# Token-major router scores and PSUM rank arithmetic in a fused attention and mixture-of-experts kernel

## The chip, the cores and the metric

One core of one Trainium2 chip runs the whole program as one launch. The metric is the device time of that launch in microseconds (us); lower is better. A kernel is timed several times, and the median stands for it. A profile is one further execution with the hardware profiler on.

## What is computed

Sparse attention in two kinds of heads, then a top-1 mixture of experts with a skip test:

```python
# attention: 8 batches, 8 heads, 576 tokens, head size 64
rel = pos[:, None] - pos[None, :]
mask_local   = (rel >= 0) & (rel < 32)                          # heads 0-3
mask_strided = (rel >= 0) & (pos[None, :] % 32 == pos[:, None] % 32)   # heads 4-7
attn = softmax(where(mask, q @ k.T / 8, -1e9)) @ v
x = attn.transpose(0, 2, 1, 3).reshape(4608, 512)
# router and experts: 8 experts, 512 -> 1024 -> 512
do_compute = x @ w_skip > 0
logits = x[do_compute] @ w_gate
e_idx  = argmax(logits); gate_w = softmax(logits)[e_idx]
y = gate_w * (relu(x @ w1[e_idx]) @ w2[e_idx])
out = x;  out[do_compute] = x + y
```

Everything is float32. The output is the attention result with the expert's result added in the rows that the skip test lets through.

## The kernel before

**Units.** The work of a batch's attention is cut into four units, `UNITS`: two of the local kind (`kind` 0, blocks of 64 tokens: five and four of them) and two of the strided kind (`kind` 1, eleven blocks of 54 tokens: three residues of 32 with 18 tokens each, in groups of six and five). A loop over `n` goes through the 32 units, `n = 4*b + pr` for batch `b` and unit `pr`. Below, (b, 2) is the iteration with `pr = 2` of batch `b`.

**One unit** passes through five steps that are Python generators; a `yield` parts what is issued on one engine from what is issued on the next:

- `qk` (line 199): TensorE computes the scores into the one PSUM tile `S`; VectorE adds the mask (line 206 for the local kind into `sm`, 208 for the strided kind into the one buffer `sms`); VectorE takes the maximum (214); GpSimd subtracts it (217).
- `tex` (237, 245): TensorE transposes, ScalarE takes the exponential out of a PSUM tile `T`, of which there are four.
- `pv` (271 to 286): TensorE multiplies with the values into the one PSUM tile `PV`; VectorE divides by the sum.
- `xpose` (313, 315): TensorE transposes the result, ScalarE copies it to `xT_[b, kind]`, one buffer for each kind. In the local kind the columns are tokens in order; in the strided kind they are `residue * 18 + token // 32`.
- `store`: the result goes to the output in DRAM.

Iteration n runs `qk` for unit n+2, `tex` for unit n, `pv` for unit n-1 and `xpose` for unit n-2, in the order that the loop body writes. The orders of TensorE, VectorE and GpSimd are those of the program; ScalarE's order is chosen by the scheduler that lays out the program.

**Routing one batch.** A batch is a group `g`, 576 tokens in five tiles of 128 (`GT`). Its steps are woven into the iterations of the next batches:

- `score` (329, 333, 334) at (b, 2) for batch b-1: for each half batch, TensorE multiplies the nine router columns `w9`, padded to 64, as the stationary operand with the transposed values as the moving one. The two kinds give two partial sums in two halves of the partitions, because their tokens are ordered differently. ScalarE copies both into `s64`, the second with a stride that restores the token order.
- `route1` at (b, 3): five TensorE transposes (349) turn `s64` token-major, ScalarE copies the one part (351), VectorE adds the other (355), and nine short VectorE operations (358 to 373) choose the expert and count.
- `route2` at (b+1, 0): TensorE prefix sums with triangular and full matrices of ones (400 to 406) give each token its rank in its expert; VectorE picks it (411, 412) into `rank_`.
- `norm`, `gates` (382 to 394): the softmax value of the chosen expert, on GpSimd, split into three bf16 parts; one reciprocal on VectorE (390).
- `hot`: four VectorE operations on five columns (430 to 433) cut the rank into quotient `hq` and remainder `hc` by 3, and two wide ones make one-hot matrices (435, 438); `mul` (446) on GpSimd multiplies one of them by the parts.
- `place` (456): TensorE adds up a table of which token goes where, and VectorE accumulates it (460, 462).

A table `plan` gives the iterations of `gates`, `hot`, `mul` and `place` for each group:

```python
plan = {x: (4 * x + 8, 4 * x + 10, 4 * x + 10, 4 * x + 12) for x in range(CB - 1)}
plan[CB - 1] = (4 * CB + 4, 4 * CB + 5, 4 * CB + 5, 4 * CB + 7)
plan[CB] = (4 * CB + 8, 4 * CB + 7, 4 * CB + 8, 4 * CB + 9)
plan[CB + 1] = (None, 4 * CB + 11, None, None)
```

With `CB = 5`, group 5 has `hot` at n = 27, `gates` and `mul` at 28 and `place` at 29. For the late batches, b = 6 and 7, `route1` and `route2` both run at (b, 3).

**The turn to the experts.** At n = 29, (7, 1), the table of groups 0 to 5 is complete; `tabled` (467 to 472) turns it into lists of tokens, and GpSimd starts an indirect gather (624) of up to 288 rows for one expert, called "e", whose weights are fetched during attention. After the loop TensorE transposes these rows (`xturn`, 646), and expert "e" starts (`ffn1a`, 691 to 695, then `ffn1`, 652 to 654) while the last batch is routed between its matrix products. Then the other seven experts follow.

Of the kernel before, what the change touches and what calls it, by code (L numbers as in the profile page):

```python
# [21 lines left out]
ST = 32  # L22
# [39 lines left out]
def _cols():  # L62
    at = 0
    for name, n in (("id", 128), ("ml", 5 * LW), ("ms", SQ), ("w8", NE), ("pk", 2 * NT), ("io", 128),
                    ("key", NE), ("e8", NE), ("cap", NE), ("ov", NOV),
                    ("eh", 24)):
        _C[name] = (at, at + n)
        at += n
    return at
# [5 lines left out]
def make_consts():  # L75
    c = np.zeros((128, C_END), np.float32)

    def put(name, a):
        c[:, slice(*_C[name])] = a

    put("id", np.eye(128))
    ml = np.zeros((128, 5, LW))
    i, w = np.arange(128)[:, None] % HP, np.arange(LW)[None, :]
    for t in range(5):
        ml[:, t] = np.where((i + 1 <= w) & (w <= i + ST) & (w >= (ST if t == 0 else 0)), 0.0, BIG)
    w = np.arange(SQ)[None, :]
# [4 lines left out]
    pk = np.zeros((128, NT, 2))  # L91
    for (a, z), o, o2 in zip(GROUPS, GOFF, GOFF[1:]):
# [13 lines left out]
def attn_moe(ctx: ExitStack, tc: tile.TileContext, q, k, v, w9d, w1d, w2d, cst, out, NB=B):  # L106
# [11 lines left out]
    ident = con["id"]  # L118
    w9 = constp.tile([128, 4, 64], F32, name="w9")
    tri = constp.tile([128, 128], BF16, name="tri")  # L120
# [10 lines left out]
    def ps(tag, n=1):  # L131
        return psum.tile([128, n, 512] if n > 1 else [128, 512], F32, name=tag, tag=tag, bufs=bufs[tag])
# [7 lines left out]
    def setup():  # L140
        fill = constp.tile([128, NE, 4], I32, name="fill")
        V.tensor_scalar(tri, con["io"], con["pk"][:, 0:1], None, op0=ALU.is_ge)
        V.memset(oneb, 1.0)
        V.memset(runs[0], 0.0)
        V.memset(s64[:, S:GT * 128], 0.0)
# [171 lines left out]

    rt_ = {}
    s64 = ap.tile([64, GT * 128], F32, name="s64")

# [3 lines left out]

    def score(b, h, tag="T"):
        p = ps(tag)
        for i in range(2):
            for kind in range(2):
                T.matmul(p[64 * kind:64 * kind + 64, 0:288], lhsT=w9[:, 2 * kind + i, :],
                         rhs=xT_[b, kind][:, i, h * 288:(h + 1) * 288], start=(i == 0), stop=(i == 1))  # L330
        yield
        at = (b - [g for g in GROUPS if g[0] <= b < g[1]][0][0]) * S
        A.copy(s64[0:32, at + h * 288:at + (h + 1) * 288], p[0:32, 0:288])
        A.copy(s64[32:64, at:at + S].rearrange("p (a r) -> p r a", r=ST)[:, 16 * h:16 * h + 16, :],
               p[64:96, 0:288].rearrange("p (r a) -> p r a", a=NA))

    def route1(g, tag="T"):
# [7 lines left out]

        sc = ps(tag)
        scv = sc[:, 0:nt * 41].rearrange("p (t c) -> p t c", c=41)
        for t in range(nt):
            T.transpose(scv[:, t, :], s64[0:41, t * 128:(t + 1) * 128], ident[:41, :41])
        s9 = sp("s9", [128, nt, 9])  # L350
        A.copy(s9, scv[:, :, 0:9])
        yield
        o = slice(GOFF[g], GOFF[g + 1])
        w8 = con["w8"].unsqueeze(1).broadcast_to([128, nt, NE])
        V.tensor_tensor(s9, scv[:, :, 32:41], s9, op=ALU.add)
        lg = s9[:, :, 1:9]
        m = sp("rm", [128, nt])
# [9 lines left out]

        V.scalar_tensor_tensor(mw, s9[:, :, 0], 0.0, mw, op0=ALU.is_gt, op1=ALU.mult)
        ohb = sp("rohb", [128, nt, NE], BF16)
# [26 lines left out]
    def route2(g, tag="T", of=None):  # L396
        nt, sp, ohb, o, _ = rt_[g]
        rk = ps(tag)
        rkv = rk[:, 0:nt * NE].rearrange("p (t e) -> p t e", e=NE)
        T.matmul(rkv, lhsT=tri, rhs=ohb, start=True, stop=False)  # L400
        yield
        for t in range(nt - 1):
            T.matmul(rkv[:, t + 1:nt, :], lhsT=oneb,
                     rhs=ohb[:, t:t + 1, :].broadcast_to([128, nt - 1 - t, NE]), start=False, stop=False)
            yield
        T.matmul(rkv, lhsT=oneb, rhs=runs[g % 2].unsqueeze(1).broadcast_to([128, nt, NE]), start=False, stop=True)
        if of is not None:
# [4 lines left out]
        V.tensor_reduce(rank_[:, o], dd, axis=AX.X, op=ALU.add)  # L412
        if of is not None:
            counted(of)
# [8 lines left out]
    def hot(g):  # L423
        o = slice(GOFF[g], GOFF[g + 1])
# [5 lines left out]
        V.tensor_scalar(q, rank_[:, o], -1.0, 1.0 / 3.0, op0=ALU.add, op1=ALU.mult)  # L430
        V.tensor_scalar(q, q, MAGIC, -MAGIC, op0=ALU.add, op1=ALU.add)
        V.tensor_tensor(c, q, pickw[:, o], op=ALU.add)
        V.scalar_tensor_tensor(c, c, -3.0, rank_[:, o], op0=ALU.mult, op1=ALU.add)
        eh = sp("heh", [24], BF16)
# [7 lines left out]
    def mul(g):  # L442
# [5 lines left out]
        hot_[g] = lo, pm  # L448

    hot_ = {}  # L450

# [391 lines left out]
    plan[CB - 1] = (4 * CB + 4, 4 * CB + 5, 4 * CB + 5, 4 * CB + 7)  # L843
    plan[CB] = (4 * CB + 8, 4 * CB + 7, 4 * CB + 8, 4 * CB + 9)
    plan[CB + 1] = (None, 4 * CB + 11, None, None)
    pool_order = ExitStack()
    pool_order.enter_context(tc.manual_schedule(engines={G.engine, T.engine, V.engine}))
    for n, (b, pr) in enumerate(units):
# [37 lines left out]
        if ranked is not None:  # L886
            rank = [route2(ranked, of=COUNTED.get(b - 1))]
# [13 lines left out]
        late = []  # L901
        if b > 0 and pr == 2:
            seq = [score(b - 1, 0), score(b - 1, 1)] + seq
        if n > 1 and not (g and pr == 2):
            seq.append(xpose(*units[n - 2]))
        run(*seq)
        if not full:
            run(*put)
        if g and pr == 3:
            norm(g[0])  # L910
        if g and pr == 2:
            late = [route1(g[0])]
        if g and pr == 3:
# [16 lines left out]
        for x, it in plan.items():  # L930
            for f, at in zip((hot, gates, mul), (it[1], it[0], it[2])):
                if at == n:
                    f(x)
# [12 lines left out]
    nr = len(GROUPS) - 1  # L946
    gates(CB + 1)
    mul(CB + 1)
    engines = ExitStack()
# [14 lines left out]
    wrest("e", 3, 5)  # L964
    run(score(NB - 1, 0), score(NB - 1, 1))
    g = ffn1("e", 2, 6)
# [140 lines left out]
def pack(inputs):  # L1107
# [23 lines left out]
    w9 = np.concatenate([np.asarray(inputs["moe_w_skip"])[:, None], np.asarray(inputs["moe_w_gate"])], axis=1)  # L1131
    w9 = np.pad(w9.reshape(4, 128, 9).transpose(1, 0, 2), ((0, 0), (0, 0), (0, 55)))
    w1 = np.asarray(inputs["moe_w1"]).reshape(NE, 4, 128, 4, 256).transpose(0, 3, 2, 1, 4).reshape(NE, 4, 128, 1024)
# [29 lines left out]
```

## Time and profile before

| quantity | value |
|---|---|
| median of 3 timed runs | 451.05 us (447.95 to 451.74) |
| time of the profiled execution | 453.04 us |
| span of the profiled execution, first to last instruction | 451.3 us |
| mean granted TensorE clock | 0.976 |
| busy: TensorE, VectorE, ScalarE, GpSimd | 412.4, 280.9, 186.4, 142.6 us |
| attention loop | from the start to about 177 us |
| experts | from about 182 us to the end |

The profile has views of one execution. The time line lists instructions by start time: start, duration, engine (PE is TensorE, PEld its weight loads, DVE is VectorE, ACT is ScalarE, POOL is GpSimd), line of the kernel, operation, output and inputs, how many instructions were merged into the row, and in brackets how long the engine had stood idle before and what ended that. A row of the windows gives the busy time of each engine in a stretch, the granted TensorE clock, the share of the DMA engines and their rate. A row of the groups sums all instructions of a line. Names lose their trailing digits, so `w9` and `s64` appear as `w` and `s`. "issue" as a releaser means that nothing that the profile shows held the engine.

### The profile page before, as it was taken

How to read it: one execution, taken by the hardware profiler on the slowest of the kernel's cores; microseconds unless marked ns; L12 is line 12 of the kernel's file. 1: busy time of each engine (PE TensorE's matmuls, PEld its weight loads, DVE VectorE, ACT ScalarE, POOL GpSimd, SP SyncE). 2: the span in 40 equal slices, each digit the busy share in tenths (PEclk: the TensorE clock that was granted, in tenths of full speed). 3: DMA queues.
4: the chain of work that ended last, by engine and by line, in shares of the span. 5: the costliest groups of instructions: out<-in, count | busy, mean ns of one | idle time of the engine just before them, and what ended most of it. 6: DMA issues, size and time to landing. Idle time of an engine off the chain costs nothing.

```text
span 451.3 us, 12196 instructions
## 1 busy us (share of the span) xinstructions
PE 412.4 (91%) x4991; PEld 370.0 (82%) x4992; DVE 280.9 (62%) x606; ACT 186.4 (41%) x370; POOL 142.6 (32%) x200
## 2 busy tenths in 40 slices
PE   5989899799889667999899999999999999999994
PEld 3866768587677556789799799999999999999984
DVE  2666798969987876781377465365484564755611
ACT  1334443436345316642443243444444444544400
POOL 2434445344454355034014327012224023200201
PEclk9799999999989979999999999999999999999999
DMA  8999989979893134515347466546566466655201
GB/s 287 388 393 315 350 276 343 326 227 352 265 377 120 43 101 153 172 69 141 91 155 212 155 201 205 167 153 187 187 199 186 152 209 192 210 159 169 61 20 42
DMA packets 51805, 90.38 MB, mean 200 GB/s; under 512 B 8251, under 2 KB 27963, under 8 KB 51745
## 3 DMA queue, kind: packets, MB, share of 16 engines
q1 hardware_dynamic: 45249, 79.19, 52.8%
q0 software_dynamic: 6496, 10.37, 8.0%
q8 instruction: 40, 0.66, 0.6%
q14 instruction: 20, 0.16, 0.1%
HBM read 75.16 MB, written 14.91 MB: 200 GB/s over the span
## 4 chain that ended last, share of the span: by engine, by line
PE 50%; DMA 2%; POOL 0%; DVE 0%; POOLq 0%; issue 0%
PE S L652 15%; PE S L654 15%; PE S L653 15%; PE PV L744 2%; DMA xg<-out_dram,tab 2%; PE T L646 1%; PE PV L786 0%; PE PV L784 0%; PE PV L785 0%; PE S L760 0%; PE S L759 0%; PE S L761 0%; POOL out_dram L732 0%; PE T L771 0%; PE S L646 0%; PE PV L646 0%
## 5 line engine op out<-in xcount | busy, mean ns | idle before, releaser
L652 PE MATMUL S<-xh,w1h 128*128 128x342 f32 (+6 forms) x248 | 78.6, 317 | 0.2 <-DVE hl L665 0.2
L654 PE MATMUL S<-xh,w1l 128*128 128x342 f32 (+6 forms) x248 | 76.7, 309 | 0.0
L653 PE MATMUL S<-xl,w1h 128*128 128x342 f32 (+6 forms) x248 | 76.6, 309 | 0.0
L732 POOL DMA_INDIRECT out_dram<-ot,tab x25 | 28.0, 1122 | 150.0 <-DVE ot L730 141.8
L652 PE MATMUL S<-hh,w2h 128*128 128x288 f32 (+5 forms) x192 | 59.4, 310 | 0.5 <-DVE hl L665 0.5
L654 PE MATMUL S<-hh,w2l 128*128 128x288 f32 (+5 forms) x192 | 58.0, 302 | 0.0
L653 PE MATMUL S<-hl,w2h 128*128 128x288 f32 (+5 forms) x192 | 57.9, 302 | 0.0
L664 ACT ACTIVATE hh<-S 128x342 fp32r<-128x342 f32 (+6 forms) x64 | 28.0, 437 | 64.0 <-PE S L654 58.3
L588 DVE TENSOR_TENSOR w1l<-raw,w1h 128x1024 fp32r<-128x1024 f32 x32 | 39.0, 1223 | 20.0 <-ACT w1h L582 20.0
L199 PE MATMUL S<-kt,qt 64*64 64x54 f32 (+1 forms) x1280 | 34.3, 247 | 14.9 <-DVE sms L208 5.0
L652 PEld LDWEIGHTS S<-xh,w1h 128*128 128x128 f32 x248 | 46.9, 189 | 0.9 <-issue 0.4
L653 PEld LDWEIGHTS S<-xl,w1h 128*128 128x128 f32 x248 | 46.8, 189 | 0.1
L654 PEld LDWEIGHTS S<-xh,w1l 128*128 128x128 f32 x248 | 46.7, 188 | 0.0
L199 PEld LDWEIGHTS S<-kt,qt 64*64 64x64 f32 x1280 | 28.3, 145 | 22.2 <-issue 7.3
L217 POOL TENSOR_TENSOR sm<-sm,mx 128x480 f32<-128x480 f32 (+1 forms) x32 | 28.5, 911 | 55.8 <-DVE mx L214 29.3
L624 POOL DMA_INDIRECT xg<-out_dram,tab x25 | 33.7, 1347 | 36.8 <-issue 14.4
L588 DVE TENSOR_TENSOR w2l<-raw,w2h 128x1024 fp32r<-128x1024 f32 x32 | 39.1, 1223 | 9.8 <-ACT w2h L582 9.6
L665 DVE SCALAR_TENSOR_TENSOR hl<-S,hh 128x342 fp32r<-128x342 f32 (+6 forms) x64 | 30.9, 483 | 17.8 <-ACT hh L664 17.7
L652 PEld LDWEIGHTS S<-hh,w2h 128*128 128x128 f32 x192 | 36.1, 188 | 0.8 <-DVE hl L665 0.8
L315 ACT COPY xT<-T 128x512 f32<-128x512 f32 (+4 forms) x56 | 22.2, 441 | 35.0 <-PE T L313 34.8
L649 DVE TENSOR_TENSOR xl<-T,xh 128x288 fp32r<-128x288 f32 (+7 forms) x30 | 13.1, 468 | 37.3 <-ACT xh L648 37.2
L653 PEld LDWEIGHTS S<-hl,w2h 128*128 128x128 f32 x192 | 36.3, 189 | 0.0
(180 smaller groups left out, 828.3 us busy)
## 6 DMA issues: line engine op xcount, KB each, us to landing
raw<-in_w_dram SPq DMA_DIRECT2D x64, 512.0 KB
vt<-in_vp_dram SPq DMA_DIRECT2D x40, 390.0 KB
qt<-in_qp_dram SPq DMA_DIRECT2D x16, 304.0 KB
kt<-in_kp_dram SPq DMA_DIRECT2D x16, 297.0 KB
out_dram<-x SPq DMA_DIRECT2D x16, 288.0 KB
kt<-in_kp_dram SPq DMA_DIRECT2D x14, 304.0 KB
qt<-in_qp_dram SPq DMA_DIRECT2D x14, 288.0 KB
out_dram<-x SPq DMA_DIRECT2D x32, 99.0 KB
```

Of the source, the lines that this page charges most:

```text
L199: T.matmul(s[HP * (i ^ j):HP * (i ^ j) + HP, j, (blk - b0) * win:(blk - b0 + 1) * win], lhsT=qt[p, j, blk * nq:blk * nq + HP], rhs=kt[p, j ...
L217: G.tensor_tensor(e[:, j], sw[:, j], mx[:, j].unsqueeze(2).broadcast_to([128, b1 - b0, win]), op=ALU.subtract)
L315: A.copy(xT_[b, kind][:, :, g * nq:(g + m) * nq].rearrange("p i (n q) -> p n i q", q=nq), t[:, 0:m * 128].rearrange("p (n i q) -> p n i q" ...
L588: V.tensor_tensor(lo, raw_.pop((key, j)), hi.bitcast(F32), op=ALU.subtract)
L624: i = G.indirect_dma_start(out=xg[:s["P"], t, :], out_offset=None, in_=out[0:last, :], in_offset=bass.IndirectOffsetOnAxis(ap=s["tab"][:s[ ...
L649: V.tensor_tensor(xl[:, c, :C], t[:, :C], xh[:, c, :C].bitcast(F32), op=ALU.subtract)
L652: T.matmul(p, lhsT=a[0], rhs=b[0], start=start, stop=False)
L653: T.matmul(p, lhsT=a[0], rhs=b[1], start=False, stop=False)
L654: T.matmul(p, lhsT=a[1], rhs=b[0], start=False, stop=stop)
L664: A.activation(s["hh"][:, f, :C], p[:, :C], AF.Relu)
L665: V.scalar_tensor_tensor(s["hl"][:, f, :C], p[:, :C], 0.0, s["hh"][:, f, :C].bitcast(F32), op0=ALU.max, op1=ALU.subtract)
L732: i = G.indirect_dma_start(out=out, in_=ot[:P], in_offset=None, bounds_check=NTOK - 1, oob_is_err=False, out_offset=bass.IndirectOffsetOnA ...
```

## The change

**Scores.** `score` and `s64` are gone. `xpose` writes the local kind into `xT_` in the strided kind's token order, with two strided copies for each group of blocks where there was one. `route1` multiplies directly: for each of the five tiles the transposed values are the stationary operand (128 columns, 64 in the last tile) and the nine router columns the moving one, four products of 128 rows summed in PSUM over the two kinds. VectorE reads the scores from PSUM. The table of token numbers `pk` follows the new order.

**Ranks.** The operations that cut the rank into quotient and remainder move from `hot` to the end of `route2`. Their intermediate values stay in the PSUM tile of the ranks, and ScalarE copies the rank and the quotient to SBUF.

**Iterations.** Group 5 has `gates`, `hot` and `mul` all at n = 27, group 6 all at n = 31 (`gates` and `mul` stood behind the loop). For b = 6 and 7 `route1` runs at the end of (b, 2) and `route2` within (b, 3).

```diff
-        pk[:, o:o2, 0] = 1 + np.arange(128)[:, None]
-        pk[:, o:o2, 1] = a * S // 64 + 2 * np.arange(o2 - o)[None, :]
+        pk[:, o:o2, 0] = 1 + (a * S + at) % 64
+        pk[:, o:o2, 1] = (a * S + at) // 64
...
     def xpose(b, pr):
...
-            A.copy(xT_[b, kind][:, :, g * nq:(g + m) * nq].rearrange("p i (n q) -> p n i q", q=nq),
-                   t[:, 0:m * 128].rearrange("p (n i q) -> p n i q", i=2, q=HP)[:, :, :, 0:nq])
+            t = t[:, 0:m * 128].rearrange("p (n i q) -> p n i q", i=2, q=HP)
+            if kind:
+                A.copy(xT_[b, 1][:, :, g * nq:(g + m) * nq].rearrange("p i (n q) -> p n i q", q=nq), t[:, :, :, 0:nq])
+                continue
+            for i in range(2):
+                A.copy(xT_[b, 0][:, i, :].rearrange("p (r n h) -> p n h r", r=ST, h=2)[:, g:g + m],
+                       t[:, :, i, :].rearrange("p n (h r) -> p n h r", r=ST))
...
-    def score(b, h, tag="T"):
-        ...
     def route1(g, tag="T"):
...
+        sc = ps(tag)[:, 0:nt * 9].rearrange("p (t c) -> p t c", c=9)
         for t in range(nt):
-            T.transpose(scv[:, t, :], s64[0:41, t * 128:(t + 1) * 128], ident[:41, :41])
-        s9 = sp("s9", [128, nt, 9])
-        A.copy(s9, scv[:, :, 0:9])
+            n = min(128, S - 128 * t)
+            if n < 128:
+                T.matmul(sc[n:128, t, :], lhsT=dummy[:, n:128], rhs=dummy[:, 0:9], start=True, stop=True)
+            for c in range(4):
+                T.matmul(sc[0:n, t, :], lhsT=xT_[g, c // 2][:, c % 2, 128 * t:128 * t + n], rhs=w9[:, c, :], start=(c == 0), stop=(c == 3))
         yield
-        V.tensor_tensor(s9, scv[:, :, 32:41], s9, op=ALU.add)
-        lg = s9[:, :, 1:9]
+        lg = sc[:, :, 1:9]
...
     def route2(g, tag="T", of=None):
...
-        dd = sp("rdd", [128, nt, NE])
+        dd = rk[:, 64:64 + nt * NE].rearrange("p (t e) -> p t e", e=NE)
+        r, a, q, c = [rk[:, 128 + 16 * i:128 + 16 * i + nt] for i in range(4)]
+        hq, hc = [ap.tile([128, GT], F32, name=n, tag=n, bufs=2) for n in ("hq", "hc")]
         V.tensor_tensor(dd, rkv, ohb, op=ALU.mult)
-        V.tensor_reduce(rank_[:, o], dd, axis=AX.X, op=ALU.add)
+        V.tensor_reduce(r, dd, axis=AX.X, op=ALU.add)
+        A.copy(rank_[:, o], r)
+        V.tensor_scalar(a, r, -1.0, 1.0 / 3.0, op0=ALU.add, op1=ALU.mult)
+        V.tensor_scalar(q, a, MAGIC, -MAGIC, op0=ALU.add, op1=ALU.add)
+        A.copy(hq, q)
+        V.tensor_tensor(c, q, pickw[:, o], op=ALU.add)
+        V.scalar_tensor_tensor(hc, c, -3.0, rank_[:, o], op0=ALU.mult, op1=ALU.add)
+        hot_[g] = hq, hc
...
     def hot(g):
-        q, c = sp("hq", []), sp("hc", [])
-        V.tensor_scalar(q, rank_[:, o], -1.0, 1.0 / 3.0, op0=ALU.add, op1=ALU.mult)
-        V.tensor_scalar(q, q, MAGIC, -MAGIC, op0=ALU.add, op1=ALU.add)
-        V.tensor_tensor(c, q, pickw[:, o], op=ALU.add)
-        V.scalar_tensor_tensor(c, c, -3.0, rank_[:, o], op0=ALU.mult, op1=ALU.add)
+        q, c = hot_[g]
...
-    plan[CB] = (4 * CB + 8, 4 * CB + 7, 4 * CB + 8, 4 * CB + 9)
-    plan[CB + 1] = (None, 4 * CB + 11, None, None)
+    plan[CB] = (4 * CB + 7, 4 * CB + 7, 4 * CB + 7, 4 * CB + 9)
+    plan[CB + 1] = (4 * CB + 11, 4 * CB + 11, 4 * CB + 11, None)
...
-        if b > CB:
-            run(*late)
-            late = []
...
-        if b > 0 and pr == 2:
-            seq = [score(b - 1, 0), score(b - 1, 1)] + seq
...
         if g and pr == 2:
             late = [route1(g[0])]
-        if g and pr == 3:
-            if b > CB:
-                run(route2(g[0], of=COUNTED.get(b)))
-            else:
-                ranked = g[0]
+        if g and pr == (2 if b > CB else 3):
+            run(*late)
+            late = []
+            norm(g[0])
+            ranked = g[0]
...
-    gates(CB + 1)
-    mul(CB + 1)
...
-    run(score(NB - 1, 0), score(NB - 1, 1))
```

More of the change, by code (lines that the diff above doesn't have):

```diff
@@ L63, in _cols @@
     at = 0
-    for name, n in (("id", 128), ("ml", 5 * LW), ("ms", SQ), ("w8", NE), ("pk", 2 * NT), ("io", 128),
+    for name, n in (("id", 128), ("ml", 5 * LW), ("ms", SQ), ("w8", NE), ("pk", 2 * NT), ("ip", 1), ("io", 128),
                     ("key", NE), ("e8", NE), ("cap", NE), ("ov", NOV),
@@ L118, in attn_moe @@
     ident = con["id"]
-    w9 = constp.tile([128, 4, 64], F32, name="w9")
+    w9 = constp.tile([128, 4, 9], F32, name="w9")
     tri = constp.tile([128, 128], BF16, name="tri")
@@ L314, in xpose @@
             yield
-            A.copy(xT_[b, kind][:, :, g * nq:(g + m) * nq].rearrange("p i (n q) -> p n i q", q=nq),
-                   t[:, 0:m * 128].rearrange("p (n i q) -> p n i q", i=2, q=HP)[:, :, :, 0:nq])
+            t = t[:, 0:m * 128].rearrange("p (n i q) -> p n i q", i=2, q=HP)
[5 more added lines that the diff above has]
+                       t[:, :, i, :].rearrange("p n (h r) -> p n h r", r=ST))
     rt_ = {}
-    s64 = ap.tile([64, GT * 128], F32, name="s64")
     def tiles(g):
         return GT
-    def score(b, h, tag="T"):
[L326 to L335, printed above, removed]
+    hot_ = {}
     def route1(g, tag="T"):
@@ L448, in mul @@
         hot_[g] = lo, pm
-    hot_ = {}
     def place(g, tag="T"):
@@ L886, in attn_moe @@
         if ranked is not None:
-            rank = [route2(ranked, of=COUNTED.get(b - 1))]
+            rank = [route2(ranked, of=COUNTED.get(b if pr else b - 1))]
             for _ in range(tiles(ranked) + 1):
@@ L930, in attn_moe @@
         for x, it in plan.items():
-            for f, at in zip((hot, gates, mul), (it[1], it[0], it[2])):
+            for f, at in zip((gates, hot, mul), it):
                 if at == n:
```

15 lines of the change are left out of this document (6 added, 9 removed).

## The prediction, made before the changed kernel ran

> **What bounds the kernel now.** First the page, for span and clock, then windows cut by batch, then the time line.
>
> ```profile
> span 451.3 us, 12196 instructions
> ...
> PEclk9799999999989979999999999999999999999999
> ...
> 63.00:82.00 19.00, 17.54 (x402) 14.02 (x396) 16.66 (x44) 8.89 (x23) 9.70 (x18) 1.00 0.95 319
> ...
> 145.00:167.00 22.00, 14.02 (x328) 11.88 (x322) 16.64 (x48) 7.69 (x18) 10.52 (x18) 0.91 0.29 80
> ```
>
> A batch takes some 19 us, the last ones 22. After the window's length the columns are PE, PEld, DVE, ACT, POOL, clock, DMA share, GB/s. In an ordinary batch PE (17.5 of 19) and DVE (16.7 of 19) share the bound: each works in a written order, and what either gains alone ends at the next wait for the other. In the stretch from 145 to 167 us PE is busy for only 14 of 22, and the clock is at 0.91: there is slack to win. The edits lie in the attention loop and in the last batch's routing; the expert phase behind is a line of matrix products that shifts as a whole.
>
> Where the batch's two engines meet, just after a rank is known, (b, 0) into (b, 1):
>
> ```profile
> 72.31 0.20 DVE L412 TENSOR_REDUCE rank<-rdd 128x5 f32<-128x40 f32 x1
> 72.42 0.82 DVE L214 TENSOR_REDUCE mx<-sms 128x12 f32<-128x648 f32 x1
> ...
> 73.39 1.42 POOL L217 TENSOR_TENSOR frame<-sms,mx 128x324 f32<-128x324 f32 x2 [0.45 <-DVE mx L214]
> ...
> 74.84 0.72 DVE L208 TENSOR_TENSOR sms<-S,cs 128x540 f32<-128x540 f32 x1 [1.32 <-POOL frame L217]
> ...
> 75.88 0.87 PEld L199 LDWEIGHTS S<-kt,qt 64*64 64x64 f32 x40 [0.17 <-DVE rc L280]
> ```
>
> DVE's maximum follows the rank directly; POOL waits for it; DVE's next mask add waits 1.32 us for POOL, because `sms` is one buffer; PE's next scores need the PSUM tile that this add frees at 75.56, and start at 75.88. From rank to scores only some 0.3 us are slack. What is put behind the rank on DVE moves all of this.
>
> **The change part by part.** *Rank arithmetic, groups 0 to 4.* It is put exactly there. Prices from the last batch, where nothing else disturbs:
>
> ```profile
> 190.22 0.20 ACT L351 COPY s<-T 128x45 f32<-128x45 f32 x1 [0.30 <-PE T L349]
> ...
> 190.51 0.20 DVE L355 TENSOR_TENSOR s<-T,s 128x45 f32<-128x45 f32 x1
> ...
> 190.97 0.20 DVE L360 TENSOR_TENSOR rd<-s,rm 128x40 f32<-128x40 f32 x1
> ...
> 191.29 0.24 ACT L362 ACTIVATE rex<-rd 128x40 f32<-128x40 f32 x1 [0.87 <-DVE rd L360]
> ...
> 193.67 0.17 DVE L430 TENSOR_SCALAR hq<-rank 128x5 f32<-128x5 f32 x1
> ...
> 194.52 0.28 DVE L435 TENSOR_TENSOR heh<-cs,hc 128x120 bf16<-128x120 f32 x1
> ```
>
> The four small operations take 0.85 us (193.67 to 194.52). ACT now copies the rank and then the quotient between them, out of the PSUM tile in which DVE goes on. No row shows ACT and DVE in one PSUM tile without ACT's result being what DVE needs. Data alone asks for no wait before the last operation, which reads the copied rank: 0 us. If DVE waits for each copy, one costs 0.12 (L360's end to ACT's start) + 0.20 + 0.09 (ACT's end to L355) = 0.41, two 0.82; and with an exponential in front of each copy (0.55 us, the group row below) two cost 1.9. I take 0.82: in the nearest row, L351 to L355, DVE starts only after ACT has left the tile. So DVE gets 1.7 us behind the rank, bounds 0.85 and 2.75, and the next scores come 1.4 us late.
>
> The Trainium skill ("PSUM — Partial Sum Buffer", section "PSUM bank collisions raise a hardware error") says that two engines must be kept apart by bank even when both only read, or use different columns; by it both copies hold DVE, and by its opposite the sum for five batches would be 4 us lower. It speaks against this part; no row of before can decide it.
>
> What `hot` loses at (b, 2):
>
> ```profile
> 78.61 2.11 PE L329 MATMUL T<-xT,w 128*64 128x288 f32 x16
> ...
> 80.98 0.41 PEld L237 LDWEIGHTS T<-cs,frame 128*118 128x118 f32 x4 [0.77 <-issue]
> ...
> 80.99 0.16 DVE L430 TENSOR_SCALAR hq<-rank 128x5 f32<-128x5 f32 x1
> ...
> 81.22 1.94 POOL L217 TENSOR_TENSOR sm<-sm,mx 128x480 f32<-128x480 f32 x2 [2.41 <-DVE hq L430]
> ...
> 81.39 0.84 DVE L432 TENSOR_TENSOR hc<-hq,pickw 128x5 f32<-128x5 f32 x1
> ...
> 82.26 0.91 DVE L433 SCALAR_TENSOR_TENSOR hc<-hc,rank 128x5 f32<-128x5 f32 x1
> ...
> 83.41 0.82 DVE L438 TENSOR_TENSOR hlo<-cs,hq 128x640 bf16<-128x640 f32 x1
> ...
> 83.56 0.38 PEld L349 LDWEIGHTS T<-cs,s 41*128 41x128 f32 x5 [0.20 <-ACT pts L245]
> ```
>
> The four took 2.2 us here, since two of them ran 0.84 and 0.91 instead of 0.17 while POOL subtracted. But POOL still subtracts: the two wide operations move into its 1.94 us and meet the same. If the last one waits for POOL's second half it ends at 84.0, for the first only, at 83.0; before it ended at 84.2. DVE gains 0.2 to 1.2, I take 0.7, and 0.23 more for the dropped L355.
>
> *Scores.* PE loses L329, 2.4 us up to the next load at 80.98, and L349, 0.4. It gains per batch 32 loads of 128 columns and 8 of 64, with nine moving columns each (two records per product). Five such loads took 0.38 us in a row, 0.06 to 0.076 each; 36 of them, the halves counted half, are 2.2 to 2.7. If such a load did not overlap at all it would cost the 138 ns of its own record, 5.0 us a batch:
>
> ```profile
> L349 PEld LDWEIGHTS T<-cs,s x40: 134/138/142, 45.1 to 189.9; 41*128 41x128 f32 x40
> ...
> L245 ACT ACTIVATE ptl<-T 96x512 f32<-96x512 f32 (+1 forms) x40 | 19.7, 545 | 34.4 <-PE T L237 34.4
> ...
> L333 ACT COPY s<-T 32x288 f32<-32x288 f32 x16 | 6.2, 387 | 26.5 <-PE T L329 26.5
> L334 ACT COPY s<-T 32x288 f32<-32x288 f32 x16 | 10.6, 663 | 0.3
> ```
>
> I take 2.45: the row of five is the same kind of load. With some 0.3 us of waiting for a `T` tile (two are now held by the local kind's transposes from (b, 2) to (b, 3), since their copies overwrite what `route1` still reads) PE's sum is even. But it moves: 2.4 us earlier at (b, 2), 2.4 later at (b, 3). That takes in most of the 1.4 us: the exponential's transposes start at 80.0 instead of 81.0, the value products behind `route1` at 84.7 instead of 84.0. DVE's own sum is 1.7 - 0.7 - 0.2 = 0.8, less what it idled. Taken together the next batch starts **0.5 us later**, five times: +2.5 us. Bounds: with no wait for the copies and the larger gain at (b, 2), 0.6 less than before, -3; with exponentials in front, 0.5 + 1.0, +7.5.
>
> ACT loses 2.1 us of copies a batch (two each of 387 and 663 ns) and pays for strided ones. 663 against 387 for the same 288 elements is nearly 1 ns more per element, if it is the stride: 1152 elements a batch, about 1.3 us with the extra starts. ACT waits 34 us for PE in L245's row alone; this is covered. If it were not, the `T` tiles would come late by as much.
>
> *The late batches.*
>
> ```profile
> 148.06 0.21 DVE L355 TENSOR_TENSOR s<-T,s 128x45 f32<-128x45 f32 x1 [2.36 <-ACT s L351]
> ...
> 153.81 0.44 DVE L430 TENSOR_SCALAR hq<-rank 128x5 f32<-128x5 f32 x1
> ...
> 155.54 0.28 DVE L435 TENSOR_TENSOR heh<-cs,hc 128x120 bf16<-128x120 f32 x1
> ...
> 159.50 2.26 POOL L217 TENSOR_TENSOR frame<-sms,mx 128x324 f32<-128x324 f32 x2 [2.85 <-DVE mx L214]
> ...
> 161.79 0.72 DVE L208 TENSOR_TENSOR sms<-S,cs 128x540 f32<-128x540 f32 x1 [1.21 <-POOL frame L217]
> ...
> 163.68 0.70 DVE L214 TENSOR_REDUCE mx<-sms 128x10 f32<-128x540 f32 x1
> ...
> 164.07 0.66 PE L456 MATMUL T<-hpm,hlo 128*128 128x120 bf16 x5 [3.58 <-POOL hpm L446]
> ...
> 164.76 0.28 DVE L462 TENSOR_TENSOR acc<-acc,T 128x120 f32<-128x120 f32 x1 [0.39 <-PE T L456]
> ...
> 167.52 3.36 PE L329 MATMUL T<-xT,w 128*64 128x288 f32 x16
> ...
> 172.61 0.97 POOL L624 DMA_INDIRECT xg<-out_dram,tab  x1 [0.30 <-issue]
> ...
> 178.85 1.33 PE L646 MATMUL T<-cs,xg 96*128 96x96 f32 x12
> ...
> DMA to landing us min/median/max: 5.0/5.7/5.8
> ```
>
> The large hole is PE's 3.58 us before `place`, waiting for group 5's `mul`, which the plan now puts an iteration earlier; it goes. Yet DVE's maximum ended at 164.38 and its accumulation started at 164.76: the hole held the token lists up by only 0.4 us. And the lists set the end of this stretch: they lead to the third gather issue at 172.61, which lands 5.0 to 5.8 later, about 178.3, and PE transposes its rows from 178.85. So the gain is what the chain of DVE gains before 164: its idle 2.36 us at 148 (`route1` now fills an earlier gap), 0.2 for L355, 1.7 for the four operations (153.81 to 155.54); against it 1.7 for their new form and 0.2 for the reciprocal that moves up. **-2.4 us.** The next wait is POOL's subtraction at 159.50; the moved `gates` and `mul`, 2.3 us from its end at 161.76 to `place`, fit into the 2.85 that POOL idled ahead of it. Bounds: 0, if the gap at (6, 2) is not there, and -4.4, if the copies cost nothing (-0.8), the hole's 0.4 is added, and the 2.26 us subtraction runs in the 1.42 of the earlier row (-0.8). PE now comes to the gathered rows some 3.6 us before they land.
>
> There a second rule speaks against the change. After the 3.58 us hole L329 took 3.36 us for what took 2.11 at 78.61, and the row of clocks has its 7 there: an idle PE lost clock. The Trainium skill ("TensorE: Matmul & The Clock Gate", section "What's actually happening") gives half rate after an idle window of about 3.4 us; the rows agree. A new hole of 3.6 us could be followed by the same loss, 1.25 us by L329's rows; I leave it out of the sum, since the hole's length is uncertain by more than the margin.
>
> *Last batch and `mul(6)`.* Score against new loads is even as above; DVE loses L355 and ACT L351, about 0.4, and gets two copies; neither is what PE waits for. 0, within 0.5.
>
> **Sum.** +2.5 - 2.4 = +0.1 on the profiled 453.04 (span 451.3 and 1.7 around it). The median lies 2.0 below that execution: **451.1 us**, taken as 451.
>
> **Rivals.** *The copies do not hold DVE* (faster): then a batch gains 0.3 instead of losing 0.5, -1.5, and the late chain gains 3.6 (2.4, 0.8 and the hole's 0.4): 446 us. For it: no data dependence; against: L351 to L355. *ACT is occupied when each copy comes due* (slower): in (b, 0), at both copies, from a wait of about 0.95 us each on; a batch loses 1.5 and the late chain only 1.3: +6, 457 us. For it: ACT's exponentials of 545 ns run in that stretch; against: ACT waits for PE most of the time. *The direct products do not overlap their loads* (138 ns each): +2.4 a batch, eight times, 470 us; against it the row of five loads. *The clock is lost before the gathered rows*: 452.3. *The change only moves waits*: PE's hole goes, and the gather still comes when it came: 453.5.
>
> **How the numbers follow.** Forecast with the last two rivals 0.56 (0.41, 0.08, 0.07), faster 0.25, occupied ACT 0.16, slow loads 0.03. A change within 1%, 4.5 us, can hardly be told from none here. The range takes the forecast's bounds and half of each side case: 444.5 to 456.5. Faster 0.25, same 0.56, slower 0.19.
>
> **What would show it.** After L412's successor, two gaps of about 0.4 us on DVE with an ACT copy in each (right), none (faster rival) or about 1 us (slower). The batch windows 0.5 us longer. No wait of PE for `hpm`; the token lists 2 to 3 us earlier relative to 145; PE waiting for `xg` before L646. The router's 40 products of a batch within 2.7 us. The prediction is wrong if an ordinary batch changes by more than 1 us, or if PE gets from the lists to the expert by another way than the gather.

## The result, and the profile after

The changed kernel takes 485.0 us (median of 4 runs, 481.9 to 486.2) against 450.5 us before (447.9 to 451.7): **1.076 times as long, 95% interval 1.069 to 1.083**, or 34.5 us more. The forecast of 451 was wrong, and so was its range. The medians of a few runs below include one or two executions that were slower at a lower clock, which their ratios leave out. The profiled execution took 485.2 us, with a span of 483.6 against 451.3 and a mean granted clock of 0.915 against 0.976.

The page of the changed kernel: the span, the row of clocks (a digit for each fortieth of the span), and two groups (busy time in all, mean ns of one, idle time before them).

```profile
span 483.6 us, 12512 instructions
...
PEclk9899797988877978577999999999999999999998
...
L348 PEld LDWEIGHTS T<-w,xT 128*128 128x128 f32 (+1 forms) x320 | 44.1, 229 | 6.4 <-ACT pts L247 5.5
L348 PE MATMUL T<-w,xT 128*128 128x9 f32 (+1 forms) x320 | 45.0, 281 | 4.4 <-ACT pts L247 3.5
```

L348 is the line of the new score products. They keep PE busy for 45.0 us, 5.6 a batch, where L329 and L349 of before took 18.2 and 4.0. The weight loads are busy for 44.1 of these 45.0: a load is in progress nearly all the time. The row of clocks, almost all 9 before, holds 8, 7 and a 5 up to its nineteenth digit (some 230 us), and is like before's behind it. The whole loss lies ahead of the point where the last batch is scored: the last score record ends at 222.5 us, in the kernel before the last of L349 at 190.2, and some 261 us follow in both.

Windows of the changed kernel, a batch each (length, PE, PEld, DVE, ACT, POOL busy, clock, DMA share, GB/s):

```profile
64.00:87.40 23.40, 21.50 (x418) 19.18 (x413) 14.86 (x45) 8.38 (x22) 8.83 (x17) 0.85 0.73 233
87.40:110.90 23.50, 21.59 (x421) 19.13 (x419) 14.87 (x44) 8.37 (x22) 9.57 (x17) 0.85 0.71 226
...
134.00:161.00 27.00, 25.09 (x422) 22.18 (x422) 14.91 (x45) 8.75 (x23) 9.49 (x17) 0.75 0.79 265
```

An ordinary batch went from 19.0 to 23.4 us. PE has 21.5 of work in it where it had 17.5, while DVE fell from 16.7 to 14.9: before, the two shared the bound, and now PE alone holds it. The waits of DVE say the same, first in the changed kernel, then in the kernel before (total us, times, longest):

```profile
DVE rc L281 <- PE PV L273: 44.4, 15, 7.9
...
DVE rm L354 <- PE T L348: 15.3, 3, 8.2
...
DVE T L412 <- ACT rank L411: 2.3, 8, 0.5
DVE T L415 <- ACT hq L414: 2.2, 8, 0.5
```

```profile
DVE rc L279 <- PE PV L271: 12.4, 12, 2.5
```

The value products are queued behind the scores on PE; DVE's wait for them grew from 12.4 to 44.4 us.

One batch on the time line of the changed kernel (start, us, what ended the idle time before it), from the ranks to the value products:

```profile
80.79 0.20 DVE L409 TENSOR_TENSOR T<-T,rohb 128x40 f32<-128x40 f32 x1
...
81.46 0.17 DVE L412 TENSOR_SCALAR T<-T 128x5 f32<-128x5 f32 x1 [0.23 <-ACT rank L411]
...
82.07 0.17 DVE L415 TENSOR_TENSOR T<-T,pickw 128x5 f32<-128x5 f32 x1 [0.23 <-ACT hq L414]
...
82.36 0.82 DVE L216 TENSOR_REDUCE mx<-sms 128x12 f32<-128x648 f32 x1
...
85.55 1.15 PE L201 MATMUL S<-kt,qt 64*64 64x96 f32 x40 [1.19 <-DVE sms L210]
...
91.66 4.34 PEld L348 LDWEIGHTS T<-w,xT 128*128 128x128 f32 x32 [0.80 <-ACT pts L247]
...
96.03 1.03 PE L348 MATMUL T<-w,xT 128*64 128x9 f32 x8
...
96.99 1.63 PE L273 MATMUL PV<-vt,pts 54*64 54x65 f32 x48
...
98.67 0.17 DVE L281 TENSOR_SCALAR rc<-PV 128x12 f32<-128x12 f32 x1 [5.87 <-PE PV L273]
```

The same places in the kernel before:

```profile
72.09 0.19 DVE L411 TENSOR_TENSOR rdd<-T,rohb 128x40 f32<-128x40 f32 x1
...
83.99 0.98 PE L271 MATMUL PV<-vt,pts 54*64 54x65 f32 x48
```

Both gaps behind the rank are there, each with an ACT copy in it; the maximum starts 1.57 us after the product `dd` (L409) instead of 0.33 (L411 to the maximum at 72.42), and PE's next scores wait 1.19 for it. Then 40 product records take 5.4 us (91.66 to 97.06), and DVE stands still for 5.87. The value products behind them take 1.63 us for what took 0.98 before.

### The profile page after: what moved, and what is told of

It reads as the page before. It is cut to its first block, busy times and chain, and to the rows that moved or that the text cites. A ratio compares the mean times of both kernels' runs of the same rounds, so it can differ in the third digit from the quotient of the medians.

```text
span 483.6 us, 12512 instructions
## 1 busy us (share of the span) xinstructions
PE 448.6 (93%) x5151; PEld 415.8 (86%) x5152; DVE 273.1 (56%) x597; ACT 180.4 (37%) x370; POOL 140.7 (29%) x200
## 5 line engine op out<-in xcount | busy, mean ns | idle before, releaser
L649 PE MATMUL S<-xh,w1h 128*128 128x342 f32 (+6 forms) x248 | 79.7, 321 | 0.5 <-DVE hl L662 0.5
L219 POOL TENSOR_TENSOR sm<-sm,mx 128x480 f32<-128x480 f32 (+1 forms) x32 | 31.3, 998 | 77.1 <-DVE mx L216 51.1
L348 PEld LDWEIGHTS T<-w,xT 128*128 128x128 f32 (+1 forms) x320 | 44.1, 229 | 6.4 <-ACT pts L247 5.5
L348 PE MATMUL T<-w,xT 128*128 128x9 f32 (+1 forms) x320 | 45.0, 281 | 4.4 <-ACT pts L247 3.5
L650 PEld LDWEIGHTS S<-xl,w1h 128*128 128x128 f32 x248 | 48.0, 193 | 0.1
L201 PE MATMUL S<-kt,qt 64*64 64x54 f32 (+1 forms) x1280 | 35.7, 259 | 13.1 <-DVE sms L210 9.0
L651 PEld LDWEIGHTS S<-xh,w1l 128*128 128x128 f32 x248 | 47.7, 192 | 0.0
L201 PEld LDWEIGHTS S<-kt,qt 64*64 64x64 f32 x1280 | 29.9, 155 | 20.4 <-DVE sms L210 10.7
L621 POOL DMA_INDIRECT xg<-out_dram,tab x25 | 30.3, 1214 | 36.2 <-issue 17.4
L322 ACT COPY xT<-T 128x256 f32<-128x256 f32 (+1 forms) x48 | 19.8, 559 | 50.4 <-PE T L348 37.1
```

The source lines that it names most:

```text
L201: T.matmul(s[HP * (i ^ j):HP * (i ^ j) + HP, j, (blk - b0) * win:(blk - b0 + 1) * win], lhsT=qt[p, j, blk * nq:blk * nq + HP], rhs=kt[p, j ...
L219: G.tensor_tensor(e[:, j], sw[:, j], mx[:, j].unsqueeze(2).broadcast_to([128, b1 - b0, win]), op=ALU.subtract)
L322: A.copy(xT_[b, 0][:, i, :].rearrange("p (r n h) -> p n h r", r=ST, h=2)[:, g:g + m], t[:, :, i, :].rearrange("p n (h r) -> p n h r", r=ST))
L348: T.matmul(sc[0:n, t, :], lhsT=xT_[g, c // 2][:, c % 2, 128 * t:128 * t + n], rhs=w9[:, c, :], start=(c == 0), stop=(c == 3))
L621: i = G.indirect_dma_start(out=xg[:s["P"], t, :], out_offset=None, in_=out[0:last, :], in_offset=bass.IndirectOffsetOnAxis(ap=s["tab"][:s[ ...
L649: T.matmul(p, lhsT=a[0], rhs=b[0], start=start, stop=False)
```

## The experiments

Ratios are to the kernel before, run beside on the same chip. "Scores", "ranks" and "moved iterations" are the three parts of the diff; "changed kernel" in an edit means that the rest is as after the change.

| run | what it has | median us | ratio, 95% interval |
|---|---|---|---|
| e1 | scores alone | 476.7 | 1.055 (1.046 to 1.064) |
| e2 | ranks and moved iterations | 459.2 | 1.018 (1.010 to 1.025) |
| e3 | changed kernel, 96 moving columns | 476.7 | 1.055 (1.046 to 1.064) |
| e4 | changed kernel, bf16 operands of the scores | 452.8 | 1.000 (0.995 to 1.005) |
| e5 | ranks alone | 464.4 | 1.029 (1.024 to 1.034) |
| e6 | moved iterations alone | 450.6 | 1.001 (0.998 to 1.004) |
| e7 | changed kernel, products in two stretches | 487.4 | 1.082 (1.079 to 1.086) |
| e8 | scores in four strips, moved iterations | 445.2 | 0.987 (0.985 to 0.990) |
| e9 | ranks alone, without ACT's copies | 457.7 | 1.011 (1.007 to 1.015) |
| e10 | scores in four strips alone | 449.5 | 0.994 (0.991 to 0.997) |
| e11 | scores alone, 96 moving columns | 466.5 | 1.031 (1.028 to 1.034) |

The theory after this profile was that the scores' loads cost their full length, and that a loss of clock comes with them. The rivals were the ranks on the path of DVE, and the moved iterations.

**e1 and e2: which part.** e1 takes the hunks of `xpose`, `route1` and `w9`, and drops `score`; e2 takes the others.

```diff
 # e1, on the kernel before
-        if b > 0 and pr == 2:
-            seq = [score(b - 1, 0), score(b - 1, 1)] + seq
+            for c in range(4):
+                T.matmul(sc[0:n, t, :], lhsT=xT_[g, c // 2][:, c % 2, 128 * t:128 * t + n], rhs=w9[:, c, :], ...)
```

> The kernel before with the score part of the change alone (transposed values as stationary operand, permuted token order, strided copies); ranks and iterations as before. Theory A: the products are bound by loading 128 float32 columns, 0.134 us a record instead of the 0.06 that was taken, and TensorE loses its clock behind them. Then this part carries all of the loss: 482 to 488 us, clock about 0.915, products of a batch 5.4 us. Rival B: the small operations on ranks, with their two copies, and the moved iterations carry a good part of it: then this kernel stands below 470.

> The change without its score part: scores as before, ranks' quotient and remainder in PSUM, other iterations for the late batches. Theory A: what the prediction had as its forecast for these two parts, 451 us, within 446 to 456, clock as before 0.97 to 0.98. Rival B: 465 or more.

The ratios are 1.055 and 1.018, and both times lie between the ranges that were expected. Together they are 7.3% of the 7.6%: the parts add up. The scores are the larger one, and the other is not free. Nor does the other cost less beside the moved scores (1.076 less 1.055) than without them (1.018), as far as intervals of 0.7 to 0.9% can tell.

**e3 and e11: the loads or the clock.** The products of L348 read 96 moving columns instead of 9; the added 87 are zeros, and nothing reads their results. The weight loads are the same. e11 does it with the scores alone.

```diff
-    w9 = constp.tile([128, 4, 9], F32, name="w9")
+    w9 = constp.tile([128, 4, 96], F32, name="w9")
```

> The changed kernel with the nine router columns padded to 96, so that each product streams 96 columns instead of 9 behind the same loads; the columns beyond 9 are zero and are not read. Theory A1 (the clock falls because TensorE streams too little while it loads): the clock stays near 0.97, the products of a batch take 4.8 us instead of 5.4, what follows them runs at full rate, some 2.3 us a batch and more in the last one are won: 466 to 470 us. Theory A2 (the clock loss has another cause): the clock stays near 0.915 and the time at 482 to 488.

> The direct scores alone, with 96 moving columns instead of 9 behind each weight load; the last 87 are zeros that nothing reads. If the clock's loss costs some 8 us whatever else stands in the kernel, 467 to 470, at a granted clock above 0.95. If the clock is lost only together with the moved ranks, 475 to 478. If the loads themselves are hidden once the clock is kept, 450 to 455.

More work, less time: e3 takes 476.7 instead of 485.0, e11 466.5 instead of e1's 476.7, half a microsecond below its first range. The clock granted over the whole run rises from 0.912 to 0.925 in the changed kernel to 0.956 to 0.960 in e3, and from 0.923 to 0.930 in e1 to 0.977 to 0.979 in e11. Windows of 1 us through the products (columns as above), of the changed kernel, then of e3:

```profile
92.66:93.66 1.00, 1.00 (x11) 1.00 (x10) 0.14 (x1) 0.00 (x0) 1.00 (x2) 1.00 1.01 334
93.66:94.66 1.00, 1.00 (x10) 1.00 (x10) 0.00 (x0) 0.00 (x0) 1.00 (x2) 0.92 1.02 360
94.66:95.66 1.00, 1.00 (x6) 1.00 (x6) 0.00 (x0) 0.00 (x0) 0.22 (x1) 0.50 1.12 353
...
99.66:100.66 1.00, 1.00 (x41) 1.00 (x44) 0.93 (x5) 0.96 (x2) 0.00 (x0) 0.50 0.14 55
...
101.66:102.66 1.00, 1.00 (x24) 0.82 (x24) 0.97 (x3) 0.75 (x2) 0.00 (x0) 1.00 0.00 0
```

```profile
93.30:94.30 1.00, 1.00 (x12) 1.00 (x10) 0.17 (x1) 0.00 (x0) 1.00 (x2) 1.00 0.90 316
94.30:95.30 1.00, 1.00 (x12) 1.00 (x10) 0.00 (x0) 0.00 (x0) 1.00 (x2) 1.00 1.12 344
95.30:96.30 1.00, 1.00 (x12) 0.91 (x11) 0.00 (x0) 0.00 (x0) 0.25 (x1) 1.00 1.18 341
```

With nine columns the clock falls to a half some 3 us into the products, although PE's records fill every one of these windows, and stays there for 6.8 us, over the value products and the next batch's work. With 96 it stays at 1.00 here. While the clock is full, the loads of 128 columns start 0.11 us apart in both traces, with 9 columns or with 96 (the counts in the windows are higher, since they include every record that reaches into one): the load sets the pace, not the columns.

e3 took 476.7 and not the 466 to 470 of its theory A1: the ranks' cost is in it, and it still loses clock there. Where the ranks hold DVE, PE waits:

```profile
84.90 1.68 PE L201 MATMUL S<-kt,qt 64*64 64x96 f32 x40 [1.93 <-DVE sms L210]
```

Around the end of this wait the clock falls to a half for 3.4 us (85.4 to 88.8). The same stands in five batches of e3, with waits of 1.91 to 2.69 us. e11 has the old ranks, and its clock is full from 15.7 to 165.8 us.

What is left of the loss in e11 is therefore the loads. By ratios, of the scores' 5.5%, 3.1% (14 us) are the loads, with whatever else this part costs, and 2.4% (11 us, from intervals of 0.9 and 0.3%) the clock. One row gives the loads at full clock, the other with the clock lost, e11 and then the changed kernel, groups of one shape:

```profile
L348 PEld LDWEIGHTS T<-w,xT 128*128 128x128 f32 x256 | 29.2, 192 | 5.6 <-ACT pts L247 5.6
```

```profile
L348 PEld LDWEIGHTS T<-w,xT 128*128 128x128 f32 x256 | 36.6, 231 | 6.4 <-ACT pts L247 5.5 <-issue 0.9
```

29.2 us by 256 is 0.114 us a load in a row; the prediction had 0.06 to 0.076. The Trainium skill ("TensorE: Matmul & The Clock Gate", section "LDWEIGHTS (loading the stationary operand)") gives a load as its columns by 1.2 in ns. For 128 columns that is 107 ns, and the trace agrees within 7%.

**e4: smaller operands.** The transposed values and `w9` are kept in bf16 for the score products alone, which rounds the scores.

```diff
-            xT_[b, kind] = ap.tile([128, 2, (S, SB * SQ)[kind]], F32, ...)
+            xT_[b, kind] = ap.tile([128, 2, (S, SB * SQ)[kind]], BF16, ...)
```

> The changed kernel with the transposed values and the router weights in bfloat16: 20 loads of two-byte columns a batch instead of 40 of float32, all else in place. It rounds the scores, so some tokens choose another expert. Theory A: the products shrink to about 1 to 1.5 us a batch, the clock stays, and the time is that of the forecast, 446 to 455 us. Rival C (not the loads but the place of the products, the two PSUM tiles held, or the strided copies): 470 or more.

452.8 us, no different from before (ratio 1.000). The 20 products of a batch are 20 records and not 40, and take 0.8 us instead of 5.4:

```profile
84.85 0.54 PE L350 MATMUL T<-w9b,xT 128*128 128x9 bf16 x16 [0.53 <-ACT pts L249]
...
85.32 0.29 PE L350 MATMUL T<-w9b,xT 128*64 128x9 bf16 x4
```

The ranks are still in it: against e2 (1.018), which has the old scores, its scores gain 1.8%. That the direct scores lose their time to the float32 products, and not to the strided copies or to their place, is shown by this, since strides and place are the same here. Its clock does not come back in full: it was granted 0.952 to 0.968 behind this ratio, and the kernel before 0.968 to 0.987.

**e5, e6 and e9: the other two parts.** e5 is the ranks alone, e6 the moved iterations alone. In e9 the four operations stand where the changed kernel has them, but DVE writes the rank and the quotient into SBUF itself:

```diff
 # e9, on e5
-        V.tensor_reduce(r, dd, axis=AX.X, op=ALU.add)
-        A.copy(rank_[:, o], r)
+        r = rank_[:, o]
+        V.tensor_reduce(r, dd, axis=AX.X, op=ALU.add)
...
-        V.tensor_scalar(q, a, MAGIC, -MAGIC, op0=ALU.add, op1=ALU.add)
-        A.copy(hq, q)
+        V.tensor_scalar(hq, a, MAGIC, -MAGIC, op0=ALU.add, op1=ALU.add)
```

> The kernel before with the ranks' part alone (quotient and remainder in PSUM with two copies by ScalarE, at the end of the rank step). Theory A: VectorE is held at each copy and the rank's successor is some 1.7 us late; with the old scores in their place TensorE has nothing to catch up with, so a batch loses 1 to 1.4 us: 456 to 462 us. Rival B: the 8 us of the ranks and iterations together come from the iterations; then this kernel is within 3 us of before.

> The kernel before with the other iterations alone. Theory A: the late batches gain what the prediction's chain gave without the new rank form, 2 to 5 us: 446 to 449 us. Rival B: the iterations are the cause of the loss: 455 or more.

> Before with the ranks' four small operations moved to where the changed kernel has them, but VectorE writes the rank and the quotient into their SBUF tiles itself: no ScalarE copy stands between them. If the position and the copies both count, the time lies between 450 and 464: VectorE gets 0.85 us behind the rank instead of 1.67 and more, so 455 to 458, and the maximum starts 1.2 us after the rank's product instead of 1.6 to 2.1. If the position alone costs the 13 us, 461 to 466. If it is the copies alone, 449 to 453.

The ranks alone cost 2.9% (13 us, above the 456 to 462 that were expected); without the copies 1.1% (5 us) are left, as expected. So the position costs 5 us and ACT's copies 8. Some of the 8 can be clock: behind this ratio e5 was granted 0.965 to 0.969, and the kernel before 0.971 to 0.987. The moved iterations cost and gain nothing alone (1.001, where 446 to 449 us were expected). e2, which has them beside the ranks, loses 1.1% less than e5 (5 us, on another chip, with intervals of 0.7 and 0.5%). Whether the moved iterations do this is not shown: they change the late batches alone, and e2's mean clock is also the higher one (0.971 against 0.966). The time line of e2, then of e9:

```profile
77.94 0.20 DVE L413 TENSOR_TENSOR T<-T,rohb 128x40 f32<-128x40 f32 x1
...
78.61 0.17 DVE L416 TENSOR_SCALAR T<-T 128x5 f32<-128x5 f32 x1 [0.23 <-ACT rank L415]
78.82 0.17 DVE L417 TENSOR_SCALAR T<-T 128x5 f32<-128x5 f32 x1
79.61 0.15 ACT L418 COPY hq<-T 128x5 f32<-128x5 f32 x1
79.79 0.17 DVE L419 TENSOR_TENSOR T<-T,pickw 128x5 f32<-128x5 f32 x1 [0.81 <-ACT hq L418]
...
80.08 0.82 DVE L214 TENSOR_REDUCE mx<-sms 128x12 f32<-128x648 f32 x1
...
83.27 0.96 PE L199 MATMUL S<-kt,qt 64*64 64x96 f32 x33 [1.74 <-DVE sms L208]
```

```profile
76.17 0.20 DVE L414 TENSOR_TENSOR T<-T,rohb 128x40 f32<-128x40 f32 x1
...
77.33 0.82 DVE L214 TENSOR_REDUCE mx<-sms 128x12 f32<-128x648 f32 x1
...
80.52 1.15 PE L199 MATMUL S<-kt,qt 64*64 64x96 f32 x40 [0.76 <-DVE sms L208]
```

From `dd` to the maximum: 0.33 us before, 1.16 in e9, 2.14 here in e2, where the second copy (79.61) started 0.6 us after its quotient (written by 78.99), behind an exponential of ACT (79.11). PE's next scores start 3.2 us after the maximum in both, and 3.5 in the kernel before: in these batches what DVE gets behind the rank reaches PE but for some 0.3 us, the slack that the prediction had.

The moved iterations do what was said of them, and something takes it back. The time line of e6:

```profile
169.50 0.97 POOL L624 DMA_INDIRECT xg<-out_dram,tab  x1 [0.30 <-issue]
...
175.33 2.13 PE L646 MATMUL T<-cs,xg 96*128 96x96 f32 x12
...
183.88 2.16 PE L329 MATMUL T<-xT,w 128*64 128x288 f32 x16
```

Against before's 172.61 the third gather is issued 3.1 us earlier, and the gathered rows are transposed at 175.33 instead of 178.85. But they take 2.13 us instead of 1.33, in the clock of these two windows of e6:

```profile
170.00:175.00 5.00, 3.39 (x54) 3.06 (x52) 4.57 (x23) 1.33 (x3) 2.08 (x7) 0.71 0.73 206
175.00:180.00 5.00, 4.45 (x24) 4.05 (x23) 3.29 (x9) 4.01 (x10) 2.26 (x4) 0.50 0.62 168
```

The clock is at a half from 172.05 on, for 10.2 us. Ahead of that PE has idled, and not for the rows but for DVE and ACT:

```profile
169.42 0.19 PE L400 MATMUL T<-rohb,tri 128*128 128x40 bf16 x1 [1.00 <-DVE rohb L370]
...
172.50 1.57 PE L271 MATMUL PV<-vt,pts 54*64 54x65 f32 x40 [1.61 <-ACT xT L315]
```

The kernel before waits 1.54 us for ACT at this place and keeps its clock there; why it is lost in e6 is not shown. The last scores start at 183.88; before, here a row of its time line, they started at

```profile
185.53 2.16 PE L329 MATMUL T<-xT,w 128*64 128x288 f32 x16
```

so half of the 3.5 us is gone by then. The medians show none of the rest.

**e7: shorter stretches.** If the clock is lost for want of streamed columns over some 3 us, two stretches with the value products between them might keep it.

```diff
+            if t == 2:
+                yield
...
+        if late:
+            next(late[0])
```

> The changed kernel with the products of a batch in two stretches: three tiles, then the value products of a unit, then the other two tiles (for batches up to 5; the last two stay in one stretch). Theory A1 (a stretch of loads longer than some 3 us costs the clock): the clock stays at 1.00 in ordinary batches, and 10 to 14 us of the 34 come back: 471 to 476 us, clock about 0.95. Theory A3 (any such stretch costs it, whatever its length): 482 to 488.

487.4 us, as theory A3 had it: no help. The row of clocks in e7 is as low as in the changed kernel:

```profile
PEclk9898797969797868577999999999999999999998
```

The first stretch still lasts 2.85 us (24 records). In two batches the clock falls about 0.2 us behind it, during the value products, and the second stretch runs its 16 records at half clock; in two others it falls in the second stretch itself.

**e8 and e10: scores with few loads.** The weights stay the loaded operand, as before, but padded to 32 columns, so that four strips of 128 tokens fill one tile; ACT copies 2 pieces instead of 4, two transposes turn them token-major, and `route1` reads them from PSUM as the changed kernel does. e8 has the moved iterations too; in both the ranks are as before.

```diff
 # e8 and e10, in place of score(b, 0) and score(b, 1)
+        for c in range(4):
+            for u in range(4):
+                T.matmul(p[32 * u:32 * u + 32, 0:128], lhsT=w9[:, c, :],
+                         rhs=xT_[b, c // 2][:, c % 2, 128 * u:128 * u + 128], ...)
```

> The kernel before with the moved iterations and with scores that keep the router columns as the stationary operand: in the permuted token order both kinds add up in one accumulation; four strips of 32 output rows take 128 tokens each and a fifth product the last 64; two copies by ScalarE, two transposes instead of five, no addition by VectorE. Ranks as before. Theory A: no load of 128 float32 columns, clock as before, TensorE's scores of a batch shrink from 2.8 to about 1.7 us and ScalarE's copies from 2.3 to about 0.5: with the iterations' gain 440 to 447 us. Rival B: the permuted order and its strided copies cost as much as is saved: 448 or more.

> The four strips of scores with few weight loads, in the place where the changed kernel has its scores, without the moved iterations of the late batches. If the place and the dropped staging copies make the gain and the moved iterations give nothing of their own, 444 to 448. If the gain came from the moved iterations together with the strips, 449 to 453.

445.2 us, 0.987 of before: e8 is 1.3% below the kernel before, the shortest time here. e10, without the moved iterations, is at 0.994, in the second of its two ranges. Its scores stand where the kernel before has them, at (b, 2), and not at the changed kernel's place of which its expectation speaks. The strips of a batch on e10's time line:

```profile
80.72 1.08 PE L336 MATMUL T<-xT,w 128*32 128x128 f32 x32
...
81.62 0.61 PE L339 MATMUL T<-xT,w 128*32 128x64 f32 x8
```

That is 1.5 us a batch (80.72 to 82.23) behind 40 loads of 32 columns, against 2.1 for L329 of before and 5.4 behind loads of 128.

## Why the prediction was wrong, and where it was right

*Failed: "36 of them, the halves counted half, are 2.2 to 2.7".* This term of the sum was mis-sized. It took its price from L349, and L349 is a transpose against the identity; "the same kind of load" was the error. A true float32 product loads 128 columns in 0.114 us in a row (e11), not in 0.076. That L349 loads 41 rows and not 128 is not the reason: before's transposes of L313 load 128, and two such loads took 0.20 us at 76.92, the second starting 0.06 after the first. A row of before had the right length, though not this pitch, since 276 and more moving columns hide it there:

```profile
L652 PEld LDWEIGHTS S<-xh,w1h 128*128 128x128 f32 x248 | 46.9, 189 | 0.9 <-issue 0.4 <-DVE hl L665 0.3
```

189 ns for this record against 138 for L349's: the loads of 128 columns that belong to products were the longer ones already there. At 0.114 the 36 loads need 4.1 us a batch, and e11's products took 4.6 (36.9 of PE by eight), not 2.45. That is 2.2 more, 17 in eight batches; e11 lost 14. The rival "do not overlap", 5.0 us a batch and 470 (471 with the 2.55 that its own numbers give), came nearest in size, and had 0.03. Its mechanism did not come: records of 0.19 us start 0.11 apart, so they do overlap.

*Missing: the clock behind the products.* The prediction weighed a lost clock for one idle hole at the end, 1.25 us. It fell instead at the scores of every batch, in stretches that PE's records fill (once, at 190.1, ahead of them), and cost 2.4% by e1 against e11.

*Failed: "the next batch starts 0.5 us later, five times".* The delay on DVE itself was right. Both copies hold it: the maximum starts 1.57 us after `dd` in the changed kernel's row and 2.14 in e2's, 1.24 and 1.81 more than before, where 1.67 was forecast with bounds of 0.85 and 2.75. Where ACT is free a copy costs less than its 0.41: DVE idles 0.23 where 0.03 lie between two of its operations, so 0.4 for both. Where ACT is not free it costs more, up to a wait of 2.5 in e2. The rule of the Trainium skill ("PSUM — Partial Sum Buffer", section "PSUM bank collisions raise a hardware error") that the prediction weighed agrees with these gaps. What failed is "that takes in most of the 1.4 us". Nothing is seen that took it in: the scores that were to make room on PE left less of it than before, and the ranks and moved iterations cost as much beside them as without (e1, e2). The ranks alone cost 13 us, 1.6 for each of eight groups. The rival "copies do not hold DVE" is refuted by the two gaps; "ACT is occupied" came too, as the 0.81 in e2's row shows.

*About right in size, and worth nothing alone: the late batches, "-2.4 us".* The hole before `place` goes, the lists come earlier (3.1 us at the gather in e6, without the new form of the ranks), and the clock is then lost before the gathered rows. This was a rival of its own with 0.08; it came, in e6 (2.13 us against 1.33) as in the changed kernel, whose twelve transposes took 2.13 as well. It did not come by the hole that the prediction named: PE waits for these rows in neither kernel.

*Right, as far as is seen: ACT's strided copies are covered.* e4 has them, at 1.49 us for 256 columns where the changed kernel's take 0.67, and is no slower than before.

By ratios the account is: loads 14 us, clock 11, position of the ranks 5, their copies 8, moved iterations -5: 33 of the 34.5. The terms come from runs on several chips, with intervals of 1 to 4 us each, and the difference lies within these. That the last term belongs to the moved iterations, and how much of the copies' 8 is clock, stays open.

## What to carry to other kernels

Price a weight load from a row of the same kind of product: a transpose's row is too cheap for a float32 product, and where the moving side has nine columns the load is the whole cost, so the operand with few columns belongs on the loaded side (e8, e10). Read the row of granted clocks beside PE's busy share, since a PE that is busy all the time can still lose its clock if it streams little, and everything behind it pays. An operation put behind the value for which the next stage waits costs its length each time, and each hop to another engine in one PSUM tile 0.2 us more here, up to 2.5 when that engine was busy.

## What was not expected of the hardware

The clock fell to 0.50 in or just behind stretches in which PE and PEld were busy in every window, with 9 moving columns behind each load of 128, 1.4 to 4.6 us after their start over the batches of the changed kernel and e1 (once it had fallen before). It fell in none of e11's eight, with 96 columns behind the same loads. In every trace here a stretch at half clock lasts 3.41 us or a multiple of it, but for the one that the end of the record cuts. The Trainium skill ("TensorE: Matmul & The Clock Gate", section "What's actually happening") lets the clock fall after an idle window of some 3.4 us. The length agrees, and the delays fit if loading alone counts as idle; that is argued from e1, e3, e7 and e11, and how activity is counted was not measured. PE need not be idle for all of such a window: in e3 a wait of 1.93 us was followed by half clock, though e2's of 1.74 was not. Nor was it tried how many columns between 9 and 96 are enough, or a first stretch shorter than e7's 2.85 us.
